# Moving the tiles of an attention and expert kernel within a partition: one unused tile for two, another place for the experts' tokens, another offset for the second layer

## The chip, the cores and the metric

The kernel runs on one core of a Trainium2 chip. The metric is the device time of one execution in microseconds; the time before is the median of three runs. The rows come from one further execution, taken by the hardware profiler.

## The reference

Eight batches of 2,496 tokens, width 256. Attention without softmax, then a mixture of eight experts of which each token takes one or none:

```python
scores = (1.0 / S) * np.matmul(z, z.transpose(0, 2, 1))       # z: 8 x 2496 x 64
x = u * np.matmul(np.maximum(scores, 0.0) ** 2, v)             # v: 8 x 2496 x 256
do_compute = x @ w_skip > 0                                    # other rows: out = x
e = argmax(x @ w_gate); g = softmax(x @ w_gate)[e]
out = x + g * (np.maximum(x @ w1[e], 0.0) @ w2[e])             # w1: 256 x 1024, w2: 1024 x 256
```

## The kernel before

Every fp32 operand of a matmul is split into a high part, rounded to the matmul's format, and a low part, the rest; a product is high x high, high x low and low x high. Everything is in fp32 sizes, 4 bytes for an element.

**Attention** (to about 1,250 us) goes over 8 batches x 5 chunks of queries (four of 512 and one of 448) x 10 steps of 256 keys, an order written out by hand (lines 32 to 38, loop from line 855). For each step `scores` (line 292, matmuls in line 302) multiplies keys `zh`, `zl` (stationary, 64 rows by 128 columns) with queries `zqh`, `zql` (moving, 512 columns); the upper and the lower 64 rows of the array hold different keys and work side by side. `straight` (line 254) copies the queries of a chunk into `zqh`, `zql` in another order; chunk 0 takes them from `zh`, `zl` themselves. ScalarE applies relu and square (lines 376, 377) into `r`, the split gives `ah` (line 386) and `al` (line 390), and `attend` (line 401, matmuls in line 419) multiplies the values `vh`, `vl` (stationary, 64 rows by 128 columns) with `ah`, `al` (moving, 512 or 448 columns) into PSUM, again two halves side by side. As the squares are symmetric, `keep` (line 310) transposes some of them into `rt` and stores them in `kept`; `recall` (line 353) loads them back five steps ahead. Loads of `raw`, `zf`, `ut`, `r` and stores of `rt` are on SP's queue.

**Experts** (from about 1,250 us): for each expert `unit` (line 663) takes up to 256 tokens in a straight part and more in the arms of a switch on the token count. `fetch` gathers tokens, `turn_pe` (line 650) turns them on TensorE and splits them into `xt` (or `xtf` in an expert's first unit, line 974). `h_part` multiplies `w1h`, `w1l` (stationary, 128 by 128) with `xt` (moving, up to 512 columns; line 692) into `psh`, splits relu of it into `hh` (line 697) and `hl` (line 698); `y_part` multiplies `hh`, `hl` (stationary) with `w2t` (moving, 256 columns; line 711).

**Where tiles lie.** A pool's tiles stand one after another within each partition, and the pools stand in the order in which they are opened (lines 71 to 79): `cpool` (constants), `vp` (tag `raw` x4; tag `v` x34, which holds `vh`, `vl`, `w1h`, `w1l`, `w2t`; 2,048 bytes each), `zp` (`zf` x3, `zh` x7, `zl` x7, `zqh` x2, `zql` x2; 2,048 each), `ap` (`r` x5, `ah` x3, `al` x3; 4,096 each), `xp` (`ut` x3, `xrow` x2; 4,096 each), `rp` (small tiles of the routing), `gp` (id lists, then `rt` x2 of 8,192 bytes), `op`. Within a pool the tags stand in the order in which they are first asked for. `hh` shares its buffers with `r`, `hl` with `ah` and `al`, `xt` with `rt`, `xtf` with `ut`, gathered tokens with `zh` and `zl`, the output tile `o` with `zqh` and `zql`. A tile that is asked for and never used only takes room: `gap` (352 bytes, line 193) and `gap2` (128 bytes, line 615). `hh`, `hl` and `xtf` use their buffers from element 80, 320 bytes in.

Of the kernel before, what the change touches and what calls it, by code (L numbers as in the profile page):

```python
# [8 lines left out]
F32 = mybir.dt.float32  # L9
F32R = mybir.dt.float32r  # L10
# [7 lines left out]
P = 128  # L18
QC = 512
# [25 lines left out]
def f32(ap):  # L45
    return ap.bitcast(F32)
# [3 lines left out]
def attn_moe(ctx, tc, zT, uT, v, wg, w1, w2, cst, pad, out):  # L50
# [20 lines left out]
    cpool = ctx.enter_context(tc.tile_pool(name="cpool", bufs=1))  # L71
    dram = ctx.enter_context(tc.tile_pool(name="dram", bufs=1, space=bass.MemoryType.DRAM))
    vp = ctx.enter_context(tc.tile_pool(name="vp", bufs=1))
    zp = ctx.enter_context(tc.tile_pool(name="zp", bufs=2))
    ap = ctx.enter_context(tc.tile_pool(name="ap", bufs=3))
    xp = ctx.enter_context(tc.tile_pool(name="xp", bufs=2))
    rp = ctx.enter_context(tc.tile_pool(name="rp", bufs=2))
    gp = ctx.enter_context(tc.tile_pool(name="gp", bufs=1))
# [111 lines left out]
    cs = cpool.tile([P, C_TRI], F32, name="cs")  # L190
    nc.scalar.dma_start(cs, cst[:, :C_TRI])
    wgs = cpool.tile([P, 2, 32], F32, name="wgs")
    cpool.tile([P, 88], F32, name="gap")
    nc.scalar.dma_start(wgs, wg)
    tri = cpool.tile([P, P], BF16, name="tri")
    trif = xp.tile([P, P], F32, name="trif", tag="xrow")
# [55 lines left out]
    zq = {}  # L252

    def straight(ci):

        b, c = ci // NQ, ci % NQ
        zq[ci] = [zp.tile([P, QC], F32R, name="zq" + x, tag="zq" + x, bufs=2) for x in "hl"]
        whole = chunks[ci][2] == QC
        for t, z in zip(zq[ci], zt[b, c]):
            zk = f32(z).rearrange("p (b a i) -> p a b i", b=4, a=4)  # L260
            for a0, a1, k, o in ((0, 4, 4, 0),) if whole else ((0, 2, 4, 0), (2, 4, 3, QC // 2)):
                to = t[:, o : o + (a1 - a0) * k * 32]
                nc.gpsimd.tensor_copy(
                    to.rearrange("p (a b i) -> p a b i", a=a1 - a0, b=k), zk[:, a0:a1, :k]
                )
# [42 lines left out]
    turned_r, puts, step = {}, [], [0]  # L308

    def keep(ci, p, r):  # L310


        b, c, j = ci // NQ, ci % NQ, p // 2
        if p % 2 == 0:
            turned_r[ci] = gp.tile([P, QC // 32, P], F32, name="rt", tag="rt", bufs=2)
        t = turned_r[ci]
        for x in range(2):
            k = (2 * p + x) % 4
            nc.vector.transpose(  # L319
                t[:, :, 32 * k : 32 * k + 32].rearrange("p (k a) i -> p a k i", k=4),  # L320
                r[:, x, :].rearrange("p (a k i) -> p a k i", a=4, k=4),
            )
        if p % 2:

            dst = kept[c, j].rearrange("(m i) k -> i m k", i=32)
            for a in range(4):
                o, w = (a * P, P) if j < NQ - 1 or a < 2 else (a * 96 + 64, 96)
                puts.append((step[0], dst[:, :, o : o + w], t[32 * a : 32 * a + 32, :, :w]))
# [35 lines left out]
    def weights(ci, p, r=None, at_end=False):  # L364
# [23 lines left out]
        def low():  # L388
            for r_, h_, l_ in views:
                nc.vector.tensor_sub(l_, r_, f32(h_))  # L390
            if own(ci, p) == 0:
                todo.setdefault(step[0] + 1, []).append(lambda: keep_half(ci, r))
            if new:
                if at_end:
                    put_off.append(lambda: keep(ci, p, r))
                else:
                    keep(ci, p, r)
# [214 lines left out]

    idts = [gp.tile([P, 2 * NSTAT, 2], I32, name="idt%d" % k) for k in range(E)]
    idt_e = gp.tile([P, 2 * NFIX, 2], I32, name="idte")
    gp.tile([P, 32], F32, name="gap2")
    xgs = {"u": [], "f": []}

    def row_tiles(t, n):
# [4 lines left out]
    xtf, xts = [], [[], []]  # L623

    def x_tiles():

        for k in range(2):
            t = gp.tile([P, 16 * P], F32R, name="xt%d" % k, tag="rt", bufs=2)
            xts[k] += [t[:, o : o + 8 * P].rearrange("p (d q) -> p d q", d=2) for o in (0, 8 * P)]

    def load_ids(t, e, n):
# [31 lines left out]
    def unit(e, hw, ids, xg, xt, fills=(), own=False, lead=3):  # L663


        W = hw * HT
        w = -(-hw // 2)
        rows_of = [min(P, W - t * P) for t in range(w)]
        xh, xl = xt
        w1h, w1l, w2t = wts[e]  # L670

        share = 1 if own else 2
        yb = [ps_acc.tile([P, 2, D], F32, name="y", tag="acc") for _ in range(-(-w // share))]
        ys = [yb[t // share][: rows_of[t], t % share, :] for t in range(w)]
        G = 2 if w < 3 else 1
        hs = []

        def h_part(p):
            ps = ps_h.tile([P, QC], F32, name="psh", tag="h")

            hh, hl = (
                ap.tile([P, 2 * QC], F32R, name="h" + c, tag=tag, bufs=k)[:, 80 : 80 + QC]
                for c, tag, k in (("h", "r", 5), ("l", "a" + "hl"[p % 2], 3))
            )
            for j in range(G):
                f = G * p + j
                m = 0
                for d in range(2):
                    k = 2 * d + f // 4
                    a, o = divmod((f % 4) * P, D)  # L690
                    for wt, x in ((w1h[k], xh), (w1h[k], xl), (w1l[k], xh)):
                        nc.tensor.matmul(  # L692
                            ps[:, j * W : (j + 1) * W], wt[:, a, o : o + P], x[:, d, :W],
                            start=(m == 0), stop=(m == 5),
                        )
                        m += 1
            nc.scalar.activation(hh[:, : G * W], ps[:, : G * W], AF.Relu)  # L697
            nc.vector.scalar_tensor_tensor(  # L698
                hl[:, : G * W], ps[:, : G * W], 0.0, f32(hh[:, : G * W]), op0=ALU.max, op1=ALU.subtract
            )  # L700
            hs.append((hh, hl))

        def y_part(p0, p1):

            fs = range(G * p0, G * p1)
            order = [(f, t) for t in range(w) for f in fs]
            for f, t in order:
                hh, hl = hs[f // G]
                tt = slice((f % G) * W + t * P, (f % G) * W + t * P + rows_of[t])
                for m, (h, k) in enumerate(((hh, 0), (hh, 1), (hl, 0))):  # L710
                    nc.tensor.matmul(  # L711
                        ys[t], h[:, tt], w2t[f][:, k, :],
                        start=(f == 0 and m == 0 and t % share == 0), stop=(f == NF - 1 and m == 2),
                        skip_group_check=True,
                    )

        np_ = NF // G
        parts = [(h_part, p) for p in range(lead)]
        for p in range(lead, np_):
            parts += [(h_part, p), (y_part, p - lead, p - lead + 1)]  # L720
        if np_ == 4:
            parts += [(y_part, k, k + 1) for k in range(np_ - lead, 2)]
            parts += [(y_part, 2, np_)]
        else:
            parts += [(y_part, np_ - lead, np_)]
        fills = dict(fills)
        for k, (f, *p) in enumerate(parts):
            f(*p)
            for g in fills.pop(k, ()):
                g()  # L730
        for k in sorted(fills):
            for g in fills[k]:
                g()
        o = zp.tile([P, 2, D], F32, name="o", tag="zqh", bufs=2)
        for t in range(w):
            if t == 2:
                o = zp.tile([P, 2, D], F32, name="o3", tag="zql", bufs=2)
            m = rows_of[t]
            ot = o[:m, t % 2, :]
            nc.vector.scalar_tensor_tensor(  # L740
                ot, ys[t], f32(ids[:m, t, 1:2]), xg[t][:m], op0=ALU.mult, op1=ALU.add
            )
            put = nc.gpsimd.indirect_dma_start(  # L743
                out=out,
                out_offset=bass.IndirectOffsetOnAxis(ap=ids[:m, t, 0:1], axis=0),
                in_=ot,
                in_offset=None,
                bounds_check=N - 1,
                oob_is_err=False,
            )  # L750
            if t:
                tc.declare_no_dep(put.ins, put0.ins, reason="the rows of a unit's tokens are distinct")
            put0 = put
# [81 lines left out]
    def early_ids():  # L835
        row_tiles("f", NFIX)
        x_tiles()
        early["cnt"] = count("cnt_e")
        load_ids(idt_e, 0, 2 * NFIX)
# [15 lines left out]
    for s, (ci, p) in enumerate(steps):  # L855
        b, q0, n = chunks[ci]
        k = s % NP
# [116 lines left out]
    def turned(e, i):  # L974
        if e and i == 0:
            if not xtf:
                for _ in range(2):
                    t = xp.tile([P, 2 * QC], F32R, name="xtf", tag="ut", bufs=3)
                    xtf.append(t[:, 80 : 80 + QC].rearrange("p (d q) -> p d q", d=2))
            return xtf  # L980
        return xts[i % 2]

# [15 lines left out]
    for e in range(E):  # L998
# [39 lines left out]
        for arm in tc.Switch(n, narms, hint="rest%d" % e):  # L1038
# [8 lines left out]
            for j, hw in enumerate(ws):  # L1047
# [6 lines left out]
                if after:  # L1054
                    xt = xts[(NFIX + j + 1) % 2]
# [72 lines left out]
```

## Time and profile before

| | |
|---|---|
| median of 3 runs | 1726.91 us (1725.61 to 1730.86) |
| the profiled execution | 1724.65 us |
| its span, first to last instruction | 1722.7 us |
| TensorE busy | 1710.2 us (99%) |
| VectorE, ScalarE, GpSimd busy | 1199.4, 1118.9, 519.6 us |
| granted TensorE clock, mean | 0.999 of full speed |

In the rows L419 is line 419 of the kernel, `acc<-ah,vh` a matmul that writes tile `acc` from `ah` and `vh`, `64*128` the stationary operand's rows and columns, and `x24` the number of instructions merged into a row. A matmul's duration contains its way through the array; the next one starts before it ends, so the distance between starts is what a matmul costs.

### The profile page before, as it was taken

To read this page: it belongs to the slowest core of one execution; us is meant where nothing else is said; L and a number is where in the kernel's file an instruction comes from. 1 tells how busy PE (TensorE), PEld (TensorE's weight loads), DVE (VectorE), ACT (ScalarE), POOL (GpSimd) and SP (SyncE) were. 2 spreads that over 40 slices of the span, in tenths; PEclk is the share of its full clock that TensorE was granted. 3 is DMA by queue.
4 is the path that set the end of the run, shared out by engine and by line. 5 is a ranking of instruction groups with operands and counts; after the bars stand their busy time and mean duration, and the time that the engine had idled before them with its cause. 6 is when DMAs were issued, how large, how long until landed. Compare 5 with 4: busy or idle time off the path is not lost.

```text
span 1722.7 us, 39254 instructions
## 1 busy us (share of the span) xinstructions
PE 1710.2 (99%) x15474; PEld 1522.8 (88%) x15474; DVE 1199.4 (70%) x1969; ACT 1118.9 (65%) x1416; POOL 519.6 (30%) x516
## 2 busy tenths in 40 slices
PE   9999999999999999999999999999999999999998
PEld 7888889988888898888889988888999999999997
DVE  7877877887887888778888778777754334344433
ACT  8877877787687778768777886877433333333321
POOL 1103203212311320231132132122355556645731
PEclk9999999999999999999999999999999999999999
DMA  5586699589868958985895799578752333323210
GB/s 191 144 212 188 154 248 285 144 209 263 246 148 235 260 165 203 273 265 135 226 250 178 197 259 276 134 216 223 212 130 76 88 95 107 91 63 97 87 43 27
DMA packets 408108, 303.25 MB, mean 176 GB/s; under 512 B 202768, under 2 KB 346001, under 8 KB 407152
## 3 DMA queue, kind: packets, MB, share of 16 engines
q1 hardware_dynamic: 393728, 276.37, 59.0%
q0 software_dynamic: 13632, 22.99, 4.7%
q8 instruction: 137, 2.24, 0.5%
q14 instruction: 179, 1.47, 0.3%
q10 hardware_dynamic: 432, 0.18, 0.0%
HBM read 184.21 MB, written 136.02 MB: 186 GB/s over the span
## 4 chain that ended last, share of the span: by engine, by line
PE 93%; DMA 3%; issue 2%; ACT 1%; DVE 1%; POOL 0%; SPq 0%; POOLq 0%; ACTq 0%; DVEq 0%
PE acc L419 59%; PE y L711 12%; PE psh L692 11%; PE ps L302 9%; DMA out<-o,idt 2%; PE psm L491 1%; PE pst L658 1%; PE ps L285 0%; DMA out<-xr 0%; DVE al L390 0%; DMA raw<-in_v 0%; ACT r L377 0%; ACT ah L386 0%; ACT r L376 0%; DVE rt L319 0%
## 5 line engine op out<-in xcount | busy, mean ns | idle before, releaser
L419 PE MATMUL acc<-ah,vh 64*128 64x512 f32 (+1 forms) x3120 | 639.6, 383 | 0.8 <-DVE ah L386 0.8
L419 PE MATMUL acc<-ah,vl 64*128 64x512 f32 (+1 forms) x3120 | 625.5, 382 | 0.0
L390 DVE TENSOR_TENSOR al<-r,ah 128x1024 fp32r<-128x1024 f32 (+1 forms) x400 | 479.0, 1205 | 134.7 <-ACT ah L386 128.3
L419 PE MATMUL acc<-al,vh 64*128 64x512 f32 (+1 forms) x3120 | 496.4, 383 | 0.4 <-DVE al L390 0.2
L590 POOL DMA_INDIRECT lst<-pair,dest x160 | 202.0, 1262 | 765.9 <-DVE dest L588 735.8
L386 ACT CAST ah<-r 128x1024 fp32r<-128x1024 f32 (+1 forms) x363 | 370.0, 1030 | 82.3 <-PE acc L419 46.9
L419 PEld LDWEIGHTS acc<-ah,vh 64*128 64x128 f32 x3120 | 325.8, 184 | 49.3 <-issue 1.4
L419 PEld LDWEIGHTS acc<-ah,vl 64*128 64x128 f32 x3120 | 326.0, 184 | 43.6 <-DVE vl L122 0.3
L419 PEld LDWEIGHTS acc<-al,vh 64*128 64x128 f32 x3120 | 309.8, 184 | 51.0 <-DVE al L390 6.3
L376 ACT ACTIVATE r<-ps 128x1024 f32<-128x1024 f32 (+1 forms) x224 | 227.9, 1018 | 132.5 <-PE ps L302 123.8
L697 ACT ACTIVATE hh<-psh 128x512 fp32r<-128x512 f32 (+2 forms) x172 | 96.4, 571 | 269.4 <-PE psh L692 254.2
L377 ACT ACTIVATE r<-r 128x1024 f32<-128x1024 f32 (+1 forms) x224 | 235.9, 1053 | 7.1
L711 PE MATMUL y<-w2t,hh 128*128 128x256 f32 (+1 forms) x1328 | 235.2, 280 | 0.0
L698 DVE SCALAR_TENSOR_TENSOR hl<-psh,hh 128x512 fp32r<-128x512 f32 (+2 forms) x172 | 110.2, 655 | 138.6 <-ACT hh L697 131.5
L319 DVE STREAM_TRANSPOSE rt<-r 128x512 f32<-128x512 f32 x304 | 197.4, 687 | 9.4 <-DMA kept<-rt 8.6
L711 PEld LDWEIGHTS y<-w2t,hh 128*128 128x128 f32 (+1 forms) x1328 | 200.6, 185 | 1.2
L711 PE MATMUL y<-w2t,hl 128*128 128x256 f32 (+1 forms) x664 | 184.2, 277 | 0.0
L692 PE MATMUL psh<-xt,w1h 128*128 128x256 f32 (+3 forms) x896 | 181.1, 300 | 1.9 <-DVE hl L698 1.9
L692 PEld LDWEIGHTS psh<-xt,w1h 128*128 128x128 f32 x896 | 140.4, 188 | 7.2 <-DVE hl L698 3.2
L692 PE MATMUL psh<-xt,w1l 128*128 128x256 f32 (+3 forms) x448 | 133.8, 299 | 0.0
L743 POOL DMA_INDIRECT out<-o,idt x77 | 76.4, 992 | 159.3 <-DVE o L740 126.4
L711 PEld LDWEIGHTS y<-w2t,hl 128*128 128x128 f32 (+1 forms) x664 | 122.6, 185 | 0.0
(197 smaller groups left out, 1735.4 us busy)
## 6 DMA issues: line engine op xcount, KB each, us to landing
kept<-rt SPq DMA_DIRECT2D x242, 256.0 KB, 4.9
r<-kept SPq DMA_DIRECT2D x90, 512.0 KB, 6.0
r<-kept SPq DMA_DIRECT2D x62, 448.0 KB, 7.2
raw<-in_v SPq DMA_DIRECT2D x80, 256.0 KB, 5.8
ut<-in_uT SPq DMA_DIRECT2D x32, 512.0 KB, 6.2
xr<-xrow SPq DMA_DIRECT2D x128, 128.0 KB, 3.7
out<-xr SPq DMA_DIRECT2D x32, 512.0 KB, 6.4
raw<-in_w SPq DMA_DIRECT2D x64, 256.0 KB, 4.0
```

Of the source, the lines that this page charges most:

```text
L302: nc.tensor.matmul(to, k[h, o : o + P], queries(ci, q, h, n), start=(m == 0), stop=(m == 2))
L319: nc.vector.transpose(t[:, :, 32 * k : 32 * k + 32].rearrange("p (k a) i -> p a k i", k=4), r[:, x, :].rearrange("p (a k i) -> p a k i", a ...
L376: nc.scalar.activation(r[:, :, :n], ps[:, :, :n], AF.Relu, scale=isc)
L377: nc.scalar.activation(r[:, :, :n], r[:, :, :n], AF.Square)
L386: (nc.scalar.copy if on_act(ci, p) else nc.vector.tensor_copy)(h_, r_)
L390: nc.vector.tensor_sub(l_, r_, f32(h_))
L419: nc.tensor.matmul(acc[t][:, :n], w[h, x, dd], a[h, x, :n], start=(first and t not in halves[:m]), stop=(last and t not in halves[m + 1 :]),)
L590: put = nc.gpsimd.indirect_dma_start(out=lst, out_offset=bass.IndirectOffsetOnAxis(ap=dest[:, t : t + 1], axis=0), in_=pair[:, t, :], in_o ...
L692: nc.tensor.matmul(ps[:, j * W : (j + 1) * W], wt[:, a, o : o + P], x[:, d, :W], start=(m == 0), stop=(m == 5),)
L697: nc.scalar.activation(hh[:, : G * W], ps[:, : G * W], AF.Relu)
L698: nc.vector.scalar_tensor_tensor(hl[:, : G * W], ps[:, : G * W], 0.0, f32(hh[:, : G * W]), op0=ALU.max, op1=ALU.subtract)
L711: nc.tensor.matmul(ys[t], h[:, tt], w2t[f][:, k, :], start=(f == 0 and m == 0 and t % share == 0), stop=(f == NF - 1 and m == 2), skip_gro ...
```

## The change

The tile `gap` of 352 bytes in `cpool` and the tile `gap2` of 128 bytes in `gp` go. An unused tile of 320 bytes is asked for in `zp` when `straight` is called for the first time, after `zf`, `zh` and `zl` and before `zqh` and `zql`. `rt` and `xt` are asked for from `xp` instead of `gp`, with the same size and number of buffers. `hh` and `hl` begin 96 elements (384 bytes) into their buffers instead of 80, and `xtf` at its buffer's start.

```diff
@@ -190,7 +190,6 @@
     wgs = cpool.tile([P, 2, 32], F32, name="wgs")
-    cpool.tile([P, 88], F32, name="gap")
     nc.scalar.dma_start(wgs, wg)
@@ -254,6 +253,8 @@
         b, c = ci // NQ, ci % NQ
+        if not zq:
+            zp.tile([P, 80], F32, name="gap", tag="gap", bufs=1)
         zq[ci] = [zp.tile([P, QC], F32R, name="zq" + x, tag="zq" + x, bufs=2) for x in "hl"]
@@ -312,7 +313,7 @@
         if p % 2 == 0:
-            turned_r[ci] = gp.tile([P, QC // 32, P], F32, name="rt", tag="rt", bufs=2)
+            turned_r[ci] = xp.tile([P, QC // 32, P], F32, name="rt", tag="rt", bufs=2)
@@ -612,7 +613,6 @@
     idt_e = gp.tile([P, 2 * NFIX, 2], I32, name="idte")
-    gp.tile([P, 32], F32, name="gap2")
@@ -625,7 +625,7 @@
         for k in range(2):
-            t = gp.tile([P, 16 * P], F32R, name="xt%d" % k, tag="rt", bufs=2)
+            t = xp.tile([P, 16 * P], F32R, name="xt%d" % k, tag="rt", bufs=2)
@@ -679,7 +679,7 @@
             hh, hl = (
-                ap.tile([P, 2 * QC], F32R, name="h" + c, tag=tag, bufs=k)[:, 80 : 80 + QC]
+                ap.tile([P, 2 * QC], F32R, name="h" + c, tag=tag, bufs=k)[:, 96 : 96 + QC]
                 for c, tag, k in (("h", "r", 5), ("l", "a" + "hl"[p % 2], 3))
@@ -976,7 +976,7 @@
                     t = xp.tile([P, 2 * QC], F32R, name="xtf", tag="ut", bufs=3)
-                    xtf.append(t[:, 80 : 80 + QC].rearrange("p (d q) -> p d q", d=2))
+                    xtf.append(t[:, :QC].rearrange("p (d q) -> p d q", d=2))
```

## Rows read from the trace of the kernel before

**Rows 1.** The page's first part (busy time, share of the span, instructions of each engine) and, of its second part, the granted clock in 40 slices.

```profile
span 1722.7 us, 39254 instructions
...
PE 1710.2 (99%) x15474; PEld 1522.8 (88%) x15474; DVE 1199.4 (70%) x1969; ACT 1118.9 (65%) x1416; POOL 519.6 (30%) x516
...
PEclk9999999999999999999999999999999999999999
```

**Rows 2.** The page's chain of waits that ended last, as shares of the span, by engine.

```profile
PE 93%; DMA 3%; issue 2%; ACT 1%; DVE 1%; POOL 0%; SPq 0%; POOLq 0%; ACTq 0%; DVEq 0%
```

**Rows 3.** The list of waits, longest first in total: TensorE's own two longest, and ScalarE's wait for recalled squares; us in total, times, longest us.

```profile
PE psh L692 <- DVE hl L698: 1.9, 3, 1.1
PE ps L302 <- ACT r L376: 1.5, 1, 1.5
...
ACT ah L386 <- DMA r<-kept: 25.3, 26, 2.0
```

**Rows 4.** The chain that ended last in order of time, pieces in attention with 512 queries; start us, us, what. The first and the last row are the first and the last of the seven pieces of 48 over 5.6 us.

```profile
204.14 5.71 PE acc L419 x48
...
500.54 0.68 PE ps L302 x6
501.22 2.72 PE acc L419 x24
...
510.74 5.69 PE acc L419 x48
...
520.51 5.44 PE acc L419 x48
...
1123.97 5.71 PE acc L419 x48
```

**Rows 5.** TensorE's instructions in order of time in a chunk of 448 queries; start us, us. Between these two rows lie nine steps of six pairs each, without a stop.

```profile
146.44 0.37 PE L419 MATMUL acc<-ah,vh 64*128 64x448 f32 x2
...
157.39 0.36 PE L419 MATMUL acc<-ah,vh 64*128 64x448 f32 x2
```

**Rows 6.** The chain in order of time, pieces in the experts. `x48` and `x24` are matmuls of 256 columns in both layers; the piece at 1290.36 has 448 columns, those at 1344.38 and 1393.10 have 512. The pieces at 1252.68 and 1629.69 are the first and the last of ten with 2.83 or 2.84 us.

```profile
1252.68 2.84 PE y L711 x24
...
1290.36 1.20 PE psh L692 x6
...
1344.38 1.37 PE psh L692 x6
...
1393.10 6.90 PE psh L692 x30
...
1477.57 5.46 PE y L711 x48
1483.03 5.44 PE psh L692 x48
...
1629.69 2.83 PE y L711 x24
```

**Rows 7.** TensorE's instructions in order of time in a unit of 512 tokens: the first matmul of the first layer and one 21 matmuls later.

```profile
1682.22 0.63 PE L692 MATMUL psh<-xt,w1h 128*128 128x512 f32 x2
...
1687.12 0.63 PE L692 MATMUL psh<-xt,w1h 128*128 128x512 f32 x2
```

**Rows 8.** Groups of instructions by line, operation, tile and shape; count, then busy us, mean ns of one, and idle us before them.

```profile
L419 PE MATMUL acc<-ah,vh 64*128 64x512 f32 x2496 | 519.5, 387 | 0.8 <-DVE ah L386 0.8
L419 PE MATMUL acc<-ah,vl 64*128 64x512 f32 x2496 | 508.8, 387 | 0.0
L419 PE MATMUL acc<-al,vh 64*128 64x512 f32 x2496 | 404.9, 388 | 0.3 <-DVE al L390 0.2
...
L711 PE MATMUL y<-w2t,hh 128*128 128x256 f32 x1248 | 221.8, 280 | 0.0
...
L711 PE MATMUL y<-w2t,hl 128*128 128x256 f32 x624 | 173.2, 277 | 0.0
...
L419 PE MATMUL acc<-ah,vh 64*128 64x448 f32 x624 | 120.1, 365 | 0.0
...
L302 PE MATMUL ps<-zqh,zh 64*128 64x512 f32 x392 | 85.2, 399 | 0.0
...
L692 PE MATMUL psh<-xtf,w1h 128*128 128x256 f32 x224 | 38.4, 276 | 0.0
```

**Rows 9.** Busy time in a stretch of attention: length; busy us (and instructions) of TensorE, its weight loads, DVE, ACT, POOL; granted clock, DMA share, GB/s.

```profile
400.00:800.00 400.00, 400.00 (x3782) 342.48 (x3780) 323.69 (x505) 309.74 (x358) 84.50 (x82) 1.00 0.79 218
```

**Rows 10.** The end of the run in order of time: TensorE's last matmul and GpSimd's last write.

```profile
1715.74 0.28 PE L711 MATMUL y<-w2t,hl 128*128 128x256 f32 x1
...
1716.82 0.97 POOL L743 DMA_INDIRECT out<-o,idt  x1 [0.44 <-POOLq L1038]
```

## The prediction

> **What bounds the kernel now.** I read the page's busy shares first, then the chain of waits as shares, then TensorE's own waits, then the chain in order of time, then the groups by shape. The shares say that TensorE is busy 1,710.2 of 1,722.7 us at full clock in every slice [rows 1], and the chain that ends last is TensorE for 93% [rows 2]. TensorE's waits on other engines add up to only a few us [rows 3]. So the time is the sum of the steps from one matmul to the next, and a change that touches no instruction can act only through the length of that step, or by letting another engine become late. The run ends with the last second-layer matmul at 1,715.74 us, an eviction, and a write issued at 1,716.82 us that lands by 1,722.7 [rows 10]; this tail moves with TensorE.
>
> The step is therefore what has to be read. In attention a piece of 24 matmuls (12 pairs; the upper and the lower 64 rows work side by side) takes 2.72 us, a piece of 48 takes 5.44, six score matmuls 0.68 [rows 4]: 226.7 ns for 512 columns. At the 2.4 GHz level that the granted clock shows, 512 columns are 213.3 ns, so 13.4 ns of each pair are something else. Between two steps of the last chunk of a batch (448 columns) 54 pairs lie in 157.39 - 146.44 = 10.95 us [rows 5], 202.8 ns a pair against 186.7 for the columns alone. In the experts, 48 matmuls of 256 columns take 5.44 us in the first layer and 5.46 in the second, 113.3 to 113.8 ns each, which is again 226.7 for 512 columns; but the second layer also runs 24 in 2.83 us, 117.9 each [rows 6].
>
> **What the change does to the places.** No instruction, wait, queue or order is changed; tiles move. I count bytes within a partition from the pools' order and sizes, each tile rounded up to 32, from the 16,512 bytes that lie ahead of cpool. Of each place I take the remainder by 512, since a 128-column weight slice is 512 bytes and nearly all slices step by 512. Before: cpool ends at 19,040, remainder 96. All tiles of vp, zp, ap and xp are whole multiples of 512, so keys, queries, values, weights, ah and al all begin at 96. The 7,488 bytes of rp, the id tiles and gap2 put rt/xt at 416; hh, hl and xtf begin 320 into their tiles, at 416. After: without the first gap keys, values and weights begin at 256; the 320-byte gap puts queries, r, ah, al and the u buffers at 64; rt/xt, now behind them, at 64; xtf at 64; hh and hl at 64 + 384 = 448. So the distance from stationary to moving operand goes from 0 to 320 in scores (zh to zqh) and attention (vh to ah), stays 320 in the first layer (w1 to xt), and goes from 192 to 320 in the second (hh to w2t). Every start was an odd multiple of 32 and becomes a multiple of 64.
>
> **Costs, part by part.** The second layer takes the first layer's distance. Its groups by shape show 280 ns mean for hh and 277 for hl, where the first layer on xtf, at 320, shows 276 [rows 8]: 1,248 x 4 + 624 x 1 = 5.6 us if all of that goes. Part of the 4 ns is the first matmul after each stop, which stays. The other end is what the chain shows of the slow pieces: 2.83 against 24 x 113.3 = 2.72, 0.11 us in each of the ten such pieces, the first and last of which stand in [rows 6]: 1.1 us. I take 2.5 us, nearer to the chain's rows, since they hold no stop.
>
> The 448-column pairs: at distance 320 six first-layer matmuls of 448 columns take 1.20 us, 200.0 ns each [rows 6], against 202.8 at distance 0. 936 pairs [rows 8] x 2.8 ns = 2.6 us. Bounds: nothing, and a loss by the 512-column rows below. I take 2.6, the row with equal columns.
>
> The 512-column pairs decide: 3,744 in attention and 392 x 3 / 2 = 588 in scores, 4,332 [rows 8]. No row shows them at 320. Two rows are near. The first layer with 256 columns at 320 has 113.3 ns, 226.7 for 512 columns: no change. The first layer with 512 columns at 320 shows 1.37 us for six, 228.3 each [rows 6], and in one stretch 21 in 1687.12 - 1682.22 = 4.90 us, 233.3 each [rows 7]: +1.6 to +6.6 ns, or +6.9 to +28.6 us over all. Attention loads two half-height weight tiles for 512 columns, one for each 256, which is the ratio of the 256-column row, so I take no change. The end below is the columns alone, 13.4 x 4,332 = 58 us.
>
> Restarts in attention: a piece of 48 that holds a stop takes 5.69 against 5.44, 0.25 us more [rows 4]. Most of that is the stop, the rest the few steps until 226.7 is reached again. Of the 33 whole pieces of 48 in the chain 7 hold one, the first and last of them 5.71 [rows 4]; of the 9,360 / 48 = 195 of the stage that makes 41. If a fifth of 0.25 goes with the new distance, 2 us; bounds nothing and 10.
>
> What moves beside TensorE: rt and xt keep two buffers of 8,192 bytes with the same users, so no buffer is waited for that wasn't. If transfers or ACT and DVE got slower by their new starts, the cover is TensorE: in attention DVE is busy 324 and ACT 310 of 400 us, and the recalled squares kept ACT waiting for 25.3 us in all without TensorE waiting for it [rows 3, 9]. DVE would have to slow by 400 / 324, 23%, to end last. I cost it at nothing; without that cover each late step would cost a stop of 0.25 us.
>
> Of the 226.7 ns a pair, 13.4 aren't columns, in three distances alike [rows 4, 6]; whatever takes them is either a part of every step or a clash that none of the three distances avoids. The Trainium skill's page "TensorE: Matmul & The Clock Gate", section "Back-to-back issue gap", gives a warm matmul its columns by 2.4 plus 2.5 ns, an estimate of 215.8 ns for 512 columns. The trace differs by 10.9 ns; by that page the excess is no part of a step, and a placement that removed it whole would take 10.9 x 4,332 = 47 us from the sum.
>
> Sum: 2.5 + 2.6 + 0 + 2 = 7.1 us less. The profiled execution took 1,724.65 us (span 1,722.7 and 1.95 around it), so it would take 1,717.6; the median of the runs is 2.26 above the profiled one, which gives 1,719.8.
>
> **Rivals.** *Nothing happens.* The same 226.7 per 512 columns at distances 0, 192 and 320 speaks for a step that doesn't depend on places at all; then the few slow pieces come from the phase at which a run of matmuls starts, and are as many afterwards. Against it: 202.8 beside 200.0. Time: 1,727 (1,722 to 1,732). The Trainium skill says as much: in "TensorE: Matmul & The Clock Gate", section "Step-by-step: what each phase is for", loading the next weights takes no read bandwidth from the running matmul. The trace doesn't settle it, as all starts here are alike by 64.
>
> *Attention takes the first layer's 512-column pattern.* Place: the 4,332 pairs; price: 1.6 to 6.6 ns each, in the middle 230.0 - 226.7 = 3.3 (30 in 6.90 us [rows 6]) x 4,332 = 14.3 us, less 5.1 for the second layer and the 448s: +9.2, 1,736 (1,729 to 1,750). It loses from the point where the pairs gain more than 5.1 / 4,332 = 1.2 ns. For it: the same columns and the same distance, and the same bytes read for each partition, one weight slice for 512 columns. Against it: the 448-column rows go the other way.
>
> *The steady step itself falls.* If part of the 13.4 ns is a clash of the two reads that the new places avoid (distance 320 everywhere, and starts that are now multiples of 64, which no row of before shows), attention gains more than all else. Half of it: 6.7 x 4,332 = 29 us, and (202.8 - 186.7) / 2 x 936 = 7.5, with the second layer 39: 1,688; ends 1,650 and 1,712. Against it: 320 alone doesn't do it in the first layer.
>
> That the change does not do what it says would be a tile order other than I count; then the distances differ and the first rival's time holds.
>
> **How the numbers follow.** Forecast 1,719.8 (1,715 to 1,725) with 0.36; nothing 0.20; attention slower 0.22; steady step falls 0.22. A difference of 0.3%, 5.2 us, is about what a measurement of this kernel can tell from no change. Faster: 0.30 of the forecast and 0.22, 0.52. Same: 0.06 + 0.18 + 0.04 = 0.28. Slower: 0.02 + 0.18 = 0.20. The range 1,680 to 1,744 leaves out the lower end of the third rival (0.08) and the upper end of the second (0.06), and some 0.05 beside.
>
> **What would show it.** In the chain of the changed kernel: pieces of 24 in attention still 2.72 us (2.74 to 2.80: second rival; under 2.70: third). In the last chunks 54 pairs in 10.80 us. In the second layer pieces of 24 at 2.72 to 2.75 and none at 2.83; the group of hh at 277 ns. Attention pieces of 48 with a stop at 5.64 or less. The first layer's 5.44 must stay, since its distance does; if it moves, the remainder by 64 matters and not the distance, and then my sum is wrong as a whole.

## The result, and the profile after

The changed kernel takes 1,740.8 us (median of 6 runs, 1,738.9 to 1,745.1) where the kernel before, beside it on the same chip, took 1,726.3. The ratio on record is 1.0079, with a 95% interval of 1.0063 to 1.0095 (the two medians alone give 1.0084). It is slower by 0.8%. The forecast was 1,719.8 and faster.

The page of the changed kernel shows the same picture as [rows 1, 2]: TensorE busy in 99% of the span, 93% of the chain, the same 15,474 matmuls. ACT and DVE are as busy as before. TensorE waits for nothing that it did not wait for before; its longest wait, for `hl`, is 4.5 us in all where 1.9 stood [rows 3], which is told below. The last line is from the list of waits, the others are from the page.

```profile
span 1743.1 us, 39254 instructions
...
PE 1727.9 (99%) x15474; PEld 1513.8 (87%) x15474; DVE 1201.9 (69%) x1969; ACT 1118.9 (64%) x1416; POOL 520.2 (30%) x516
...
PE 93%; DMA 3%; issue 2%; ACT 1%; DVE 1%; POOL 0%; SPq 0%; ACTq 0%; POOLq 0%; DVEq 0%
...
PE psh L692 <- DVE hl L698: 4.5, 4, 2.1
```

So the steps from one matmul to the next have grown. In the chain in order of time (start us, us, what), attention with 512 queries, the pieces that answer to [rows 4] are longer: 24 matmuls 2.75 us instead of 2.72, 48 take 5.49 instead of 5.44, that is 229 ns a pair instead of 226.7.

```profile
502.08 2.75 PE acc L420 x24
...
515.12 5.68 PE acc L420 x48
...
524.93 5.49 PE acc L420 x48
```

In a chunk of 448 queries (TensorE's instructions in order of time, as [rows 5]) the steps are shorter: nine times six pairs take 160.80 - 150.00 = 10.80 us, 200.0 ns a pair where 202.8 stood.

```profile
150.00 0.36 PE L420 MATMUL acc<-ah,vh 64*128 64x448 f32 x2
...
160.80 0.36 PE L420 MATMUL acc<-ah,vh 64*128 64x448 f32 x2
```

In the experts (the chain, as [rows 6]) a piece of 48 of the second layer takes 5.65 us where 5.46 stood, and so does one of the first layer, though its distance is the same as before. Only now and then is there a first-layer piece of the old length, here the one at 1549.69; the second layer that follows it has already lost it, and from there on both layers are slow again.

```profile
1268.00 5.65 PE y L711 x48
1273.65 5.65 PE psh L692 x48
...
1549.69 5.44 PE psh L692 x48
...
1555.57 5.66 PE y L711 x48
1561.22 5.66 PE psh L692 x48
```

The groups by shape (count, then busy us and mean ns of one) say it in sum: attention with 512 columns went from 387 to 390 and 389 ns a matmul, with 448 from 365 to 362, the second layer from 280 and 277 to 282 and 280, the first layer on xtf from 276 to 278 [rows 8].

```profile
L420 PE MATMUL acc<-ah,vh 64*128 64x512 f32 x2496 | 512.5, 390 | 0.8 <-DVE ah L387 0.8
L420 PE MATMUL acc<-ah,vl 64*128 64x512 f32 x2496 | 501.3, 389 | 0.0
...
L711 PE MATMUL y<-w2t,hh 128*128 128x256 f32 x1248 | 227.2, 282 | 0.0
L711 PE MATMUL y<-w2t,hl 128*128 128x256 f32 x624 | 174.5, 280 | 0.0
L420 PE MATMUL acc<-ah,vh 64*128 64x448 f32 x624 | 118.7, 362 | 0.0
...
L692 PE MATMUL psh<-xtf,w1h 128*128 128x256 f32 x224 | 39.5, 278 | 0.0
```

A group's mean counts the overlap with the next matmul, so from here on I use **mean steps**: from TensorE's instructions in order of time, the time from the start of a pair (or of a matmul of full height) to the start of the next, averaged over all steps of a shape except **stops**, the steps over 252 ns (512 columns), 223 (448) or 138 (256). Number of steps times difference of means is what a shape adds:

```
ns                    steps   before    after   change us
attention, 512 cols    3744    227.4    229.2        +6.5
attention, 448 cols     936    203.2    200.1        -2.9
scores, 512 cols        618    228.0    229.7        +1.0
first layer, 256       1296    113.8    117.2        +4.4
second layer, 256      1991    114.8    117.4        +5.2
smaller shapes                                       -0.2
sum                                                 +14.0
```

0.0079 x 1,727 is 13.6 us, so the steps account for the change within the interval. The two profiled executions differ by more, 1743.1 - 1722.7 = 20.4 us: 3.0 us lie in the first 40 us (the matmul that starts at 40.2 us before starts at 43.2), in this run with a granted clock of 0.94 over the first 60 us where the run of before has 1.00. That comes and goes between executions: e4, the changed kernel moved up by 32 bytes, has 1.00 there, and e9, the kernel before but for its 448-column chunks, has 0.94. Another 3.2 us lie at the start of the second expert, where TensorE waits 1.86 us for `hl` instead of 0.28 and its next two pieces take 2.29 and 2.16 us instead of 1.47 and 1.38; the granted clock of that stretch is 0.98. Whether the longer wait goes with the change is not settled: e2, the changed kernel with the old second layer, waits 0.28 us there, e1, e3 and e4, whose second layer lies as the changed kernel's, 1.3 to 1.7, but e9, whose experts lie as before, 3.26, with the same slow pieces after it. I don't count it as the change's. 14.0 + 3.0 + 3.2 makes 20.2, a little better than it should: the sum leaves out that attention's stops take 1.2 us less (below) and the experts' other stops about 1 us more. The two stretches in the windows view (length; busy us of TensorE, its weight loads, DVE, ACT, POOL; granted clock, DMA share, GB/s):

```profile
0.00:60.00 60.00, 56.40 (x482) 44.75 (x484) 41.68 (x53) 47.65 (x56) 4.87 (x15) 0.94 0.46 148
...
1220.00:1300.00 80.00, 78.14 (x693) 73.17 (x690) 52.71 (x127) 32.69 (x61) 36.20 (x34) 0.98 0.59 158
```

### The profile page after: what moved, and what is told of

It reads as the page before. It is cut to its first block, busy times and chain, and to the rows that moved or that the text cites. A ratio compares the mean times of both kernels' runs of the same rounds, so it can differ in the third digit from the quotient of the medians.

```text
span 1743.1 us, 39254 instructions
## 1 busy us (share of the span) xinstructions
PE 1727.9 (99%) x15474; PEld 1513.8 (87%) x15474; DVE 1201.9 (69%) x1969; ACT 1118.9 (64%) x1416; POOL 520.2 (30%) x516
## 3 DMA queue, kind: packets, MB, share of 16 engines
q14 instruction: 179, 1.47, 0.3%
## 4 chain that ended last, share of the span: by engine, by line
PE 93%; DMA 3%; issue 2%; ACT 1%; DVE 1%; POOL 0%; SPq 0%; ACTq 0%; POOLq 0%; DVEq 0%
PE acc L420 59%; PE y L711 12%; PE psh L692 11%; PE ps L303 9%; DMA out<-o,idt 2%; PE psm L492 1%; PE pst L658 1%; PE ps L286 0%; DMA out<-xr 0%; DMA raw<-in_v 0%; ACT r L378 0%; ACT ah L387 0%; ACT r L377 0%; DVE al L391 0%; DVE rt L320 0%
## 5 line engine op out<-in xcount | busy, mean ns | idle before, releaser
L420 PE MATMUL acc<-ah,vh 64*128 64x512 f32 (+1 forms) x3120 | 631.2, 384 | 0.8 <-DVE ah L387 0.8
L420 PE MATMUL acc<-ah,vl 64*128 64x512 f32 (+1 forms) x3120 | 616.7, 383 | 0.0
L420 PE MATMUL acc<-al,vh 64*128 64x512 f32 (+1 forms) x3120 | 491.4, 383 | 0.3 <-DVE al L391 0.2
L591 POOL DMA_INDIRECT lst<-pair,dest x160 | 205.7, 1286 | 768.6 <-DVE dest L589 738.5
L420 PEld LDWEIGHTS acc<-ah,vh 64*128 64x128 f32 x3120 | 314.6, 185 | 57.1 <-DVE ah L387 1.3
L420 PEld LDWEIGHTS acc<-ah,vl 64*128 64x128 f32 x3120 | 314.6, 185 | 50.7 <-DVE vl L122 0.3
L420 PEld LDWEIGHTS acc<-al,vh 64*128 64x128 f32 x3120 | 301.8, 185 | 57.2 <-DVE al L391 4.3
L377 ACT ACTIVATE r<-ps 128x1024 f32<-128x1024 f32 (+1 forms) x224 | 228.0, 1018 | 141.6 <-PE ps L303 133.6
L711 PE MATMUL y<-w2t,hh 128*128 128x256 f32 (+1 forms) x1328 | 240.9, 282 | 0.0
L711 PEld LDWEIGHTS y<-w2t,hh 128*128 128x128 f32 (+1 forms) x1328 | 202.8, 185 | 1.3
L692 PE MATMUL psh<-xt,w1h 128*128 128x256 f32 (+3 forms) x896 | 185.1, 303 | 4.5 <-DVE hl L698 4.5
(197 smaller groups left out, 1722.7 us busy)
```

Source lines behind the costliest of these rows:

```text
L377: nc.scalar.activation(r[:, :, :n], ps[:, :, :n], AF.Relu, scale=isc)
L420: nc.tensor.matmul(acc[t][:, :n], w[h, x, dd], a[h, x, :n], start=(first and t not in halves[:m]), stop=(last and t not in halves[m + 1 :]),)
L591: put = nc.gpsimd.indirect_dma_start(out=lst, out_offset=bass.IndirectOffsetOnAxis(ap=dest[:, t : t + 1], axis=0), in_=pair[:, t, :], in_o ...
L692: nc.tensor.matmul(ps[:, j * W : (j + 1) * W], wt[:, a, o : o + P], x[:, d, :W], start=(m == 0), stop=(m == 5),)
L711: nc.tensor.matmul(ys[t], h[:, tt], w2t[f][:, k, :], start=(f == 0 and m == 0 and t % share == 0), stop=(f == NF - 1 and m == 2), skip_gro ...
```

## Experiments

**Theory 1:** the distance from stationary to moving operand sets the pattern of steps, of 512, 448 and 256 columns each in its own way; for 256 columns there are two levels, 113.4 and 117.8 ns, of which distance 192 in the second layer brings back the short one while 320 keeps whichever it finds, and the first layer inherits it. **Theory 2:** the starts' remainder by 64 (odd multiples of 32 before, multiples of 64 after) is what counts. This is what the prediction said a moved first layer would mean.

### One part at a time

**e1**, the kernel before with the second layer alone at 320:

```diff
-    ap.tile([P, 2 * QC], F32R, name="h" + c, tag=tag, bufs=k)[:, 80 : 80 + QC]
+    ap.tile([P, 2 * QC], F32R, name="h" + c, tag=tag, bufs=k)[:, 48 : 48 + QC]
```

> The kernel before with one part of the change alone: hh and hl begin 192 bytes into their tiles in place of 320, so that only the second layer's distance (w2t's start less hh's, mod 512) goes from 192 to 320; all else, the odd multiples of 32 too, is as before. If that distance sets the step (theory 1): the second layer goes from 114.8 to about 117.4 ns per 256 columns and carries the slow state into the first layer (113.8 to about 117.2 ns), together 5 + 4.5 us, so about 1736 us (1.0055 of before); attention stays at 226.7 to 227.5 ns. If the starts' remainder by 64 is what counts (theory 2): no change, 1726 us, both layers at 114 to 115 ns.

Measured 1.0031 (1.0018 to 1.0044), 5.4 us. Second layer 116.1 ns, first layer 116.2, attention 227.4 and scores 228.0 as before. Theory 1 in direction, at 0.6 of the size: the chain shows long stretches at either level. The first layer takes the level of the second layer just before it; the level changes across a turning of the next tokens (0.44 us on TensorE), as between 1363.82 and 1369.90, and survives another, as between 1375.35 and 1381.23.

```profile
1311.36 5.65 PE y L711 x48
1317.01 5.65 PE psh L692 x48
...
1363.82 5.65 PE psh L692 x48
...
1369.90 5.45 PE y L711 x48
1375.35 5.44 PE psh L692 x48
...
1381.23 5.45 PE y L711 x48
```

Here every start is an odd multiple of 32, as before, and w1 and xt lie where they lay: the first layer's loss of 3.0 us comes through the second layer alone.

TensorE's instructions in order of time say where a level can change. I take the unbroken runs of at least 20 matmuls of 256 columns, without a stop and without other matmuls between them, first and second layer alike, and compare a run's start with its end. In the five kernels whose experts lie at 320 or 64 (the changed one, e1, e3, e4, e10) there are 46 such runs each, and not one of the 230 changes its level. Every change lies at a break. At the breaks the kernels differ, though both layers lie at 320 in them: in e1 8 breaks lead from the long step to the short and 8 the other way, in the changed kernel 4 and 4, with far fewer runs short, 4 of 46 against 18.

**e2**, the changed kernel with the second layer back at 192 (`[:, 96 : 96 + QC]` becomes `[:, 0 : QC]`):

> The changed kernel with the second layer's distance put back: hh and hl begin at the start of their tiles, 192 instead of 320 from w2t, all starts still multiples of 64. Theory 1: both layers of the experts return to 113.8 to 114.8 ns per 256 columns, 9 to 10 us less than the changed kernel: about 1731 us, 1.003 of before; attention stays at 229.2 ns (512 columns) and 200.1 (448). Theory 2: as the changed kernel, 1741 us, both layers at 117 ns.

Measured 1.0037 (1.0026 to 1.0048), 7.2 us less than the changed kernel's 1.0079. Attention stays at 229.2 and 200.1. Both layers come to 115.3 ns, for the second most of the way, for the first a little over half. In most experts the pieces of 60 matmuls near the start bring the short step back and two units keep it; a third runs at 117.8 in both layers, and after it the second layer comes down again.

```profile
523.25 5.49 PE acc L420 x48
...
1426.47 5.47 PE y L711 x48
1431.94 5.44 PE psh L692 x48
...
1437.83 5.66 PE y L711 x48
1443.48 5.66 PE psh L692 x48
```

So 192 brings the short step back mostly, not always. Why it is lost in the third unit here and not in the kernel before stays open.

**e3**, the changed kernel with keys to queries back at 0; the 320 bytes stand ahead of rt, so that the experts keep 320:

```diff
-        if not zq:
-            zp.tile([P, 80], F32, name="gap", tag="gap", bufs=1)
...
+        if not turned_r:
+            xp.tile([P, 80], F32, name="gap_rt", tag="gap_rt", bufs=1)
...
-                ap.tile([P, 2 * QC], F32R, name="h" + c, tag=tag, bufs=k)[:, 96 : 96 + QC]
+                ap.tile([P, 2 * QC], F32R, name="h" + c, tag=tag, bufs=k)[:, 48 : 48 + QC]
...
-                    xtf.append(t[:, :QC].rearrange("p (d q) -> p d q", d=2))
+                    xtf.append(t[:, 80 : 80 + QC].rearrange("p (d q) -> p d q", d=2))
```

> The changed kernel without the 320 bytes between keys and queries (they stand ahead of rt instead): scores and attention have distance 0 again, at starts of remainder 256; both layers of the experts stay at 320, all starts multiples of 64. Theory 1: attention returns to 226.7 to 227.5 ns for 512 columns and 202.8 to 203.2 for 448, scores to 228; the experts stay at 117 ns: about 4.6 us less than the changed kernel, 1736 us. Theory 2: attention stays at 229.2 and 200.1 ns, 1741 us.

Measured 1.0053 (1.0037 to 1.0070), 4.5 us less than the changed kernel. Attention 227.3 and 203.2 ns, scores 228.0: the steps of before, at starts of 256 where before they were at 96. The experts stay at 117.2 and 117.4.

```profile
523.65 5.44 PE acc L420 x48
...
1431.42 5.65 PE y L711 x48
1437.07 5.66 PE psh L692 x48
```

**e4**, the changed kernel with everything 32 bytes up:

```diff
     wgs = cpool.tile([P, 2, 32], F32, name="wgs")
+    cpool.tile([P, 8], F32, name="gap_c")
```

> The changed kernel with 32 unused bytes at the end of its constants: every operand begins 32 bytes later, at an odd multiple of 32, as before the change, and every distance is the changed kernel's. Theory 1: nothing changes, 1741 us, 229.2, 200.1 and 117 ns. Theory 2: towards the kernel before, 1726 us if it is all of the cause, with 226.7 ns in attention and 114 in the experts.

Measured 1.0069 (1.0053 to 1.0086), the changed kernel's time within the two intervals. Attention 229.3 and 200.1, experts 116.9 and 116.9. Theory 2 has fallen. (`ident`, with which tokens are turned, lies ahead of the new gap and does not move, so "every operand" leaves out the turning. The 16,512 bytes that the prediction counts ahead of cpool stand in no row; no distance depends on them, and a shift by 32 bytes tests theory 2 whatever they are.)

```profile
522.18 5.49 PE acc L421 x48
...
1431.27 5.66 PE y L712 x48
1436.93 5.66 PE psh L693 x48
```

### All distances alike

**e5** (0), **e6** (128), **e7** (192), **e8** (256) and **e10** (64) change sizes and offsets alone (at 0 the gap goes out); for 128:

```diff
-            zp.tile([P, 80], F32, name="gap", tag="gap", bufs=1)
+            zp.tile([P, 32], F32, name="gap", tag="gap", bufs=1)
...
-    ap.tile([P, 2 * QC], F32R, name="h" + c, tag=tag, bufs=k)[:, 96 : 96 + QC]
+    ap.tile([P, 2 * QC], F32R, name="h" + c, tag=tag, bufs=k)[:, 64 : 64 + QC]
```

> The changed kernel with every gap taken out and hh, hl at the start of their tiles: scores, attention and both layers of the experts all have distance 0. The distance theory: attention and scores as in the kernel before (226.7 ns steady, 227.4 mean for 512 columns, 203.2 for 448). For the experts at 0 it gives no number by itself; if 256 columns follow what 512 do at the same distance (226.7 is twice 113.3), both layers settle at 113.4 ns after each turning: about 1722 us, 4 less than before. The rival, that the two states of the experts are kept from wherever they came, whatever the distance unless it is 192: parts of the stage stay at 117.9, 1727 to 1737 us.

> All four distances at 128. A scan, to see whether the step is one function of the distance: attention steps of 512 columns between 226.7 (as at 0) and 229.2 ns (as at 320), of 448 between 200.1 and 203.2, experts between 113.4 and 117.9; 1720 to 1745 us. If 512 and 256 columns go together, a steady 226.7 in attention comes with 113.4 in the experts.

> All four distances at 192, where the second layer of the kernel before relaxes to 113.4 ns. If the distance and its complement (512 - 192 = 320) act alike, attention is as in the changed kernel (229.2 and 200.1 ns), and only the experts gain: about 1727 to 1731 us. If a distance at which 256 columns relax is also one at which 512 hold 226.7, attention is as before and the first layer relaxes too: about 1722 us.

> All four distances at 256, half a weight slice. A scan like the one at 128: attention between 226.7 and 229.2 ns (512 columns) and 200.1 and 203.2 (448), experts between 113.4 and 117.9; 1720 to 1745 us. If the gain at 448 columns is an average over half-slice shifts (448 is three and a half slices), then 448 shows the same step at 0 and at 256.

> All four distances at 64 in place of the changed kernel's 320. If the steps repeat modulo 256: as the changed kernel everywhere, 229.2 and 200.1 ns in attention, both layers at 117 to 117.4 with parts at 113.4, 1.006 to 1.009 of before. If the repeat is 512: other steps, no number given.

**e11** and **e12** put scores and attention, first layer and second layer at 32, 96, 224 and at 224, 288, 160 in the same way (by the gap, a second gap ahead of rt, and the offsets of hh, hl and xtf):

> A finer scan, with scores and attention at 32, the first layer at 96 and the second at 224. If the step changes smoothly with the distance, each lies between its neighbours: attention between 226.7 and 228.9 ns at 512 columns and between 200.1 and 203.2 at 448; the first layer between the 117.8 or 113.4 kept at 64 and the 118.6 at 128; the second between 114.1 (192) and 119.5 (256).

> The finer scan's other half: scores and attention at 224, the first layer at 288 (32 modulo 256), the second at 160. Smooth: attention between 226.7 (256) and 233.3 ns (192) at 512 columns and 202.2 to 203.2 at 448; the first layer between the states kept at 320 and the 120 at 256; the second between 114.1 (192) and 118.5 (128). If one of these settles at 113.4 ns from any entry, a layout better than both kernels exists there.

Mean steps in ns, the sum that these and the smaller shapes make against the kernel before (steps x difference, as above), and the measured ratio as us of 1,727. In the measurements of e5 to e12 the kernel before took 1,734.7 to 1,734.8 us, so their times are compared by the ratio; their sums use the steps of before from the trace shown here and lie up to 5.9 us above what was measured:

```
       distances of      attention    scores  first  second    sum  measured
       att/1st/2nd       512    448      512    256     256     us  (95% interval of the ratio)
before   0/320/192     227.4  203.2    228.0  113.8   114.8
after  320/320/320     229.2  200.1    229.7  117.2   117.4  +14.0  +13.6 (1.0063-1.0095)
e1       0/320/320     227.4  203.6    228.0  116.2   116.1   +5.8   +5.4 (1.0018-1.0044)
e2     320/320/192     229.2  200.1    229.8  115.3   115.3   +7.5   +6.4 (1.0026-1.0048)
e3       0/320/320     227.3  203.2    228.0  117.2   117.4   +9.1   +9.2 (1.0037-1.0070)
e4     320/320/320     229.3  200.1    229.7  116.9   116.9  +13.1  +11.9 (1.0053-1.0086)
e5       0/  0/  0     227.3  203.2    228.1  120.0   119.3  +16.8  +12.8 (1.0051-1.0098)
e8     256/256/256     227.3  203.2    228.1  120.0   119.4  +17.1  +15.4 (1.0072-1.0106)
e10     64/ 64/ 64     229.1  200.1    229.7  117.3   117.4  +13.9  +11.9 (1.0041-1.0096)
e6     128/128/128     232.6  203.7    232.6  119.0   118.6  +37.5  +31.6 (1.0166-1.0200)
e7     192/192/192     233.3  202.2    233.3  117.8   114.1  +28.3  +25.7 (1.0132-1.0166)
e11     32/ 96/224     233.3  204.7    233.2  119.9   118.2  +42.1  +38.2 (1.0195-1.0247)
e12    224/288/160     233.3  204.0    233.2  116.9   118.0  +37.0  +31.9 (1.0158-1.0211)
e9   0, 64 for 448     227.4  200.2    227.9  114.2   115.2   -1.9   -1.2 (0.9978-1.0008)
```

Part of what the sums have too much is in the stops. Between the same two matmuls of attention (the 501st and the 11,701st of the run) the stops of 512-column pairs cost, above the mean step, 4.1 to 4.8 us in all where the distance is 0 or 256, 3.1 at 320 and 64, and 1.9 to 2.2 at 32, 128, 192 and 224: the longer the step, the less a stop adds.

Three things can be read here. 0 and 256 are alike, and so are 64 and 320, in every column: for these two pairs the steps repeat with the distance modulo 256. They don't change smoothly with it: attention is at its floor at 0, near it at 64, and at 32, which lies between, it has the 233.3 of 192 and 224. And 512 and 256 columns do not go together: at 0 attention is best while the experts are worst, 120 ns. e5 lost its expectation of 1,722 by this, and e7 the hope that a distance at which the second layer relaxes is good for attention, or that 192 acts as 320 does. The ranges expected of e6 and e8 missed too: attention's 232.6 ns at 128 lies above 229.2, the experts' 119.0 at 128 and 120.0 at 256 above 117.9; and the smooth course expected of e11 and e12 does not hold for attention at 32. The expert columns of e11 and e12 have a different distance in each layer, and one layer can pass its level on, so they are not read as the property of one distance. The chain of e5:

```profile
522.47 5.44 PE acc L418 x48
...
1424.95 5.76 PE y L709 x48
1430.71 5.76 PE psh L690 x48
```

And of e7, where at the same distance of 192 the second layer comes down to 5.46 and the first goes up to 5.66 each time anew:

```profile
503.63 2.80 PE acc L420 x24
...
1446.79 5.66 PE psh L692 x48
...
1452.89 5.46 PE y L711 x48
1458.35 5.66 PE psh L692 x48
```

### The one good part alone

**e9**, the kernel before with the 448-column chunks alone at 64:

```diff
             for a0, a1, k, o in ((0, 4, 4, 0),) if whole else ((0, 2, 4, 0), (2, 4, 3, QC // 2)):
+                o += 0 if whole else 16
...
-            return zq[ci][k][h, :n]
+            s = 16 * (n < QC)
+            return zq[ci][k][h, s : s + n]
...
-            views.append([x[:, :, :n] for x in (r, ah, al)])
+            s = 16 * (n < QC)
+            views.append([r[:, :, :n]] + [x[:, :, s : s + n] for x in (ah, al)])
...
-                acc[t][:, :n], w[h, x, dd], a[h, x, :n],
+                acc[t][:, :n], w[h, x, dd], a[h, x, s : s + n],
```

> The kernel before, but in the chunks of 448 columns queries, ah and al begin 16 columns (64 bytes) into their 512-column tiles, so that these chunks alone have distance 64; everything else lies as before. If the steps repeat with the distance modulo 256 (0 and 256 were alike), 64 is what 320 was in the changed kernel: 936 pairs of attention go from 203.2 to 200.1 ns (-2.9 us), some 65 of the scores from 203.6 to 200.4 (-0.2), nothing else moves: about 0.998 of before. If the repeat is 512, no step need change or 448 goes up to the 203.8 ns seen at 128: 1.000.

The step did what was expected: from 148.51 to 160.51 lie ten times six pairs, 200.0 ns each, and the mean went from 203.2 to 200.2, 2.8 us less.

```profile
148.51 0.36 PE L423 MATMUL acc<-ah,vh 64*128 64x448 f32 x2
...
160.51 0.36 PE L423 MATMUL acc<-ah,vh 64*128 64x448 f32 x2
```

The time did not show it: 0.9993, 0.9978 to 1.0008. In the profiled run the experts gave back 1.2 us by the level that they happened to be at, and what is left, 1.9 us of 1,727, lies inside the interval. It is neither shown to be faster nor excluded.

## Why the prediction was wrong

**"The second layer takes the first layer's distance", -2.5 us.** This step failed first. The sign was wrong: the second layer lost 5.2 us. I had read the first layer's 5.44 [rows 6] as what distance 320 does. It was the level that the second layer, at 192, had handed over, and 320 only kept it; with the second layer at 320 too, no run of matmuls comes back to the short step once it is at the long one, except where it is broken off and begins anew. e1 shows this on the kernel before, e2 in reverse. The bounds, 1.1 to 5.6 of gain, held no loss, because a neighbour's steady row was taken for a property of its place.

**"The first layer's 5.44 must stay."** It went to 5.65 and cost 4.4 us more, a term that the sum didn't have. I had said that this would mean that the remainder by 64 matters and not the distance. That reading was wrong as well: e4 moved every start to an odd multiple of 32 without giving the time back, and e1 lost the first layer without moving any operand of it.

**"The 512-column pairs", no change.** Attention and scores went up 1.8 and 1.7 ns a pair, together 7.5 us. e3 undoes the distance and gets all of it back. The step that failed is the choice between the two near rows: the 256-column row at 320 was taken because of its equal count of weight tiles for each 512 columns, and that row wasn't fixed. The second rival had the right row, the first layer with 512 columns, and the right sign; its price of 3.3 ns was nearly twice the 1.8 measured, which its lower end, 1.6, comes close to.

**"The 448-column pairs", -2.6 us.** Right: -2.9. Here a row with equal columns at the new distance was at hand.

**Restarts, -2 us.** In part, and for another reason. A piece of 48 with a stop takes 5.68 against 5.69 [rows 4], while one without a stop went from 5.44 to 5.49. Above the mean step the stops of 512-column pairs cost 3.1 us where 4.3 stood, 1.2 less; but the sum counted on a steady step that stays, and over all layouts a stop adds less where the steps are longer. The right sign is luck.

**What moves beside TensorE,** nothing: right, DVE and ACT are as busy as they were.

Put together, the second rival's 14.3 - 5.1 should have been 7.5 - 3.1 + 9.6 = 14.0, where 3.1 is the 448-column part of attention and scores. Its time, 1,736 (1,729 to 1,750), was the nearest, by two errors that partly cancel. The third rival, that the steady step falls, finds nothing: in none of the fourteen layouts is attention's mean under 227.3.

The first rival leant on the Trainium skill, "TensorE: Matmul & The Clock Gate", section "Step-by-step: what each phase is for", by which loading the next weights takes nothing from the running matmul's reads. The runs speak against a step that doesn't depend on places: with the same instructions in the same order, attention's mean step goes from 227.3 to 233.3 ns by the place of the moving operand against the weights. Whether it is the reads that meet, no run shows.

**What stays open:** why a distance costs what it does. That the step repeats every 256 bytes and depends on both operands' places speaks for the two reads meeting each other, but no run measured that. Nor is it settled what level a run of an expert's matmuls takes when it begins after a break (64, 320); e1, e4 and the changed kernel, all at 320, differ in how much of the stage is at either. One candidate was never moved by itself: the gathered tokens lie at three different distances from `ident` in these three kernels, and most breaks are turnings, which multiply one by the other. e3 and e10, which share the changed kernel's distance there, also share its share of short runs, 4 and 3 of 46.

## What to carry to other kernels

When TensorE is the bound and its matmuls come back to back, look at the steps between starts by shape; where they differ from columns / clock, the places of the two operands in a partition are a term of the time, here up to 2.2% of it (e11). Take a price only from a row of the same shape at the same distance, and before taking a steady row as the property of its place, ask what came before it: a phase can be inherited. Move one pair of operands at a time, and judge by the mean step of each shape, which tells 1 ns from nothing where the time of a run can't.

## What the runs showed of the hardware

- The step of a run of fp32 matmuls depends on the distance of the moving from the stationary operand within a partition, and two pairs of distances 256 bytes apart (0 and 256, 64 and 320) give the same step: 64-row pairs of 512 columns 227.3 ns at 0 and 256, 229.2 at 64 and 320, 232.6 at 128, 233.3 at 32, 192 and 224. Shifting both operands by the same 32 or 160 bytes changes nothing in attention (e4 against the changed kernel, e3 against the kernel before).
- Which distance is best depends on the columns: for 448 it is 64 (200.1 against 203.2 at 0); for 256 the longest steps are at 0 and 256 (119.3 to 120.0).
- 256-column matmuls at 64 and 320 have two levels, 113.4 and 117.8 ns. In 230 unbroken runs of five kernels the level never changed within a run, nor from one layer to the next; it changed only where a run was broken. At 192 the second layer mostly falls back to 113.4 within a run, and the first rises to 117.8 (e7).
